# Bucketed attention and a feed-forward block on one core: an earlier row of maxima, a first operand loaded once, and conversions at other places

## The chip, the cores and the metric

The kernel runs on one core of a Trainium2 chip. Its engines work side by side and meet at semaphores: TensorE (PE, with its weight loads PEld), VectorE (DVE), ScalarE (ACT), GpSimd (POOL), and SyncE (SP), which here does nothing but issue DMAs. Each engine, and each DMA queue, takes its instructions in the order in which the program lists them. The metric is the device time of one execution in microseconds, lower is better.

## What is computed

Attention in which a query sees only the keys of its own hash bucket, and then a feed-forward block on its result:

```python
q, k, v: [4, 8, 768, 64] * 0.1;  proj: [64, 6];  w_in: [512, 2048];  w_out: [2048, 512]
bucket(x) = sum over n of 2**n * (x @ proj > 0)[n]
scores = where(bucket(q)[:, None] == bucket(k)[None], q @ k.T / 8, -1e9)
scores = scores - max(scores, -1);  attn = exp(scores)
attn = attn / (sum(attn) + 1e-9);   x = (attn @ v), as [4 * 768, 512]
h = x @ w_in
g = where(h >= 1, h, where(h <= -1, 0, (h + 1)**2 / 4))
out = g @ w_out
```

Everything is float32. Most products are made from two parts of the operands: a rounded high part and the low part that is left.

## The kernel before

**Two stages.** The first is attention over 32 heads (4 batches of 8), in 16 pairs that share tiles; the second is the feed-forward block (FFN).

**Units.** Each head has 12 units (`NU`): two halves of 384 queries by six blocks of 128 keys. The loop over `g` runs through 32 x 12 units. In unit `g` PE makes the scores of one block of keys (`s_unit`, lines 391 and 392: two matmuls, of which the second takes in the bucket bits and the row of maxima), ACT makes two exponentials of them (line 400 the rounded one `ph`, line 405 the exact one), DVE or POOL subtracts to get the low part `pl` (`lo_unit`, helper `sub` on line 39), and PE makes the products with V four units later (`LAG`, `pv_unit`, lines 424, 426 and 428). In between, PE makes the scores of a head two heads on for its maximum (`max_mm`, line 323; DVE reduces them in `max_red`, line 327).

**Three sets of tiles.** Pair `pr` uses `T1[pr % 3]` and `T2[pr % 3]`. What a pair needs is made in the even head two pairs ahead: `cast_h` and `low_h` (POOL) split the raw operand, `move` (four DMAs on SP, part 0 to 3) copies halves between partitions, `bits_mm` (PE, line 221) and `bits_cmp` (DVE) make the bucket bits, `bits_scale` (POOL) and `bits_put` (four DMAs) bring them to rows 0 to 6 of `T2`.

**The row of maxima.** Row 7 of `T2` holds each query's negated maximum, clamped. For head `hd + 2` it is made in head `hd + 1`: `max_clamp` (POOL, lines 357 and 359), `max_tr` (a PE transpose, line 368), `max_put` (an ACT copy to `te`, line 373, and two DMAs on SP, line 375 to `T2` and line 377 to `e_d` in DRAM). The first score unit of head `hd + 2` reads that row in its second matmul (line 392).

**Order.** Beside the units everything is put at a unit by hand: `at(g, fn, ...)` adds a task to unit `g`, tasks of one unit run in the order in which they were added, after the unit's own work. The weights' tasks are added first, then those of the first operand, then attention's. The loop over `hd` in `attention` adds the steps named above.

**Weights.** The weights come as 64-bit words and are turned into float32 by `word_steps` (a load; ACT's `rebias`; DVE's `tail`, `shifted` and `signed`). `conv` puts these at units. Those of `w_in` are turned into the blocks that the FFN needs during attention and stored in `wc`. Of the 16 blocks of `w_out` eleven are converted during attention too, stored in DRAM (`wd`, line 108) and fetched again (`get`, line 112), and five are converted in the FFN.

**The FFN** works in four blocks (batches) of 56 products (8 x 7, an algorithm with seven products in place of eight). Product `k` is six matmuls (line 960), then one step on DVE or ACT that sums it up, the activation (ACT lines 811, 812; DVE lines 817, 818, issued by `due(1, k)`), its high and low part (`g_hi`, `g_lo`), and matmuls with `w_out` from a queue (line 856). Tasks stand in `prep[k]` (ahead of the product's matmuls) and `post[k]` (behind them).

**The FFN's operand.** It is the attention's result, which goes to DRAM (`xd`) head by head, plus sum of V, normalized. For block 0 it is made during attention by three objects of class `FirstX`: `fx[0]` and `fx[1]` are the left and right half (192 columns each) of the even column blocks, `fx[2]` the odd ones at full width (384). Each has four pieces, each with these steps: `load` (a DMA of the raw piece, from `xd`), `rows` (two DMAs of the per-head rows, `er`), `fill` (one DVE instruction, line 743: row times `sv` plus raw), `norm` (POOL, line 748: times the second row), and then `sums`, `hi` and `lo`. For the later blocks `x_plan` places the same steps in the FFN.

## Time and profile before

| | before |
|---|---|
| time, median of 3 runs | 1008.0 us (1003.87 to 1008.73) |
| time of the profiled execution | 1006.24 us |
| its span, first to last instruction | 1004.4 us |
| mean granted clock of TensorE | 0.989 |
| busy: PE, PEld | 964.9 us (96%), 888.1 us (88%) |
| busy: DVE, ACT, POOL | 748.2 us (74%), 685.7 us (68%), 375.1 us (37%) |
| DMA | 174.37 MB in 85209 packets, 174 GB/s on average |

How to read the rows below: a row of a time line has the start and the duration in us, engine, source line, operation, and what is written from what (out<-in); SPq is the SP queue, whose rows are issues of DMAs, not their transfers; several alike in a row are merged (x3). In brackets stands how long the engine was idle before, and what ended that. A row of waits says who waited for whom: us in total, times, the longest. A row of windows has the window, its length, then the busy time of PE, PEld, DVE, ACT and POOL with their instruction counts, the granted clock, the busy share of the DMA engines and GB/s. Matmuls are pipelined: one is recorded about twice as long as the distance from one to the next. Attention lasts to about 490 us of the span; the FFN follows.

### The profile page before, as it was taken

What the parts mean: (1) busy time and instruction counts of PE and PEld (TensorE: products, weight loads), DVE (VectorE), ACT (ScalarE), POOL (GpSimd) and SP (SyncE); (2) the same over time, 40 slices, a digit from 0 to 9 for tenths busy, and PEclk for the clock granted to TensorE, in tenths of its full rate; (3) what the DMA queues carried; (4) which work ended last, traced back from release to release, by engine and by line L of the source; (5) the groups of instructions that cost most, each with busy time, mean ns of one, the idle gap of its engine ahead of it and who ended that gap; (6) DMA issues with size and microseconds to landing.
All of it is one profiled execution on the core that took longest, in us unless ns stands there. A gap on an engine that the chain in (4) does not pass through costs nothing.

```text
span 1004.4 us, 15651 instructions
## 1 busy us (share of the span) xinstructions
PE 964.9 (96%) x5002; PEld 888.1 (88%) x5002; DVE 748.2 (74%) x1311; ACT 685.7 (68%) x1510; POOL 375.1 (37%) x500
## 2 busy tenths in 40 slices
PE   8999999989999979989999999999999999999998
PEld 7899999988999979879888878888998889988896
DVE  8778888877888868878577898677766677755554
ACT  7889899978889968878655656545555454554444
POOL 8767778857779857876400000000000000000000
PEclk9999999989999989999999999999999999999999
DMA  6766766868776666664485764946448465454431
GB/s 165 188 170 169 207 182 174 250 179 248 199 202 166 184 212 175 186 205 136 144 228 167 217 218 126 260 134 195 118 134 245 133 179 148 134 168 116 116 105 63
DMA packets 85209, 174.37 MB, mean 174 GB/s; under 512 B 13524, under 2 KB 35656, under 8 KB 84104
## 3 DMA queue, kind: packets, MB, share of 16 engines
q1 hardware_dynamic: 84858, 173.34, 60.8%
q8 instruction: 40, 0.66, 0.3%
q14 instruction: 41, 0.34, 0.1%
q10 hardware_dynamic: 270, 0.04, 0.0%
HBM read 116.35 MB, written 30.46 MB: 146 GB/s over the span
## 4 chain that ended last, share of the span: by engine, by line
PE 68%; DVE 9%; ACT 9%; DMA 7%; issue 2%; POOL 1%; SPq 1%; ACTq 0%; DVEq 0%; POOLq 0%
PE y L856 23%; PE h L960 20%; DMA t<-te 5%; PE smax L323 5%; PE s L392 4%; PE o L424 4%; PE o L428 4%; PE o L426 4%; PE s L391 4%; ACT ph L400 2%; PE o L221 2%; DVE nm L327 2%; ACT pf L405 1%; ACT s L405 1%; DVE t L817 1%
## 5 line engine op out<-in xcount | busy, mean ns | idle before, releaser
L400 ACT ACTIVATE ph<-s 128x384 fp32r<-128x384 f32 x380 | 190.5, 501 | 52.0 <-PE s L392 45.3
L327 DVE TENSOR_REDUCE nm<-smax 128x1 f32<-128x768 f32 x189 | 180.2, 954 | 39.9 <-PE smax L323 38.8
L39 DVE TENSOR_TENSOR pl<-s,ph 128x384 fp32r<-128x384 f32 x256 | 138.8, 551 | 31.7 <-ACT s L405 27.5
L817 DVE SCALAR_TENSOR_TENSOR t<-t 128x384 f32<-128x384 f32 x128 | 71.4, 558 | 108.9 <-ACT z L812 108.8
L39 POOL TENSOR_TENSOR pl<-pf,ph 128x384 fp32r<-128x384 f32 x128 | 130.5, 1023 | 55.0 <-ACT pf L405 52.1
L392 PE MATMUL s<-t 128*128 128x384 f32 x384 | 132.3, 345 | 17.0 <-DMA t<-te 16.9
L424 PE MATMUL o<-ph,va 128*128 128x386 f32 x384 | 132.1, 344 | 5.1 <-DVE rw L83 4.9
L428 PE MATMUL o<-pl,va 128*128 128x386 f32 x384 | 131.7, 343 | 1.2 <-DVE pl L39 1.2
L391 PE MATMUL s<-t 128*128 128x384 f32 x384 | 132.0, 344 | 0.0
L426 PE MATMUL o<-ph,vb 128*128 128x386 f32 x384 | 131.6, 343 | 0.0
L405 ACT ACTIVATE s<-s 128x384 f32<-128x384 f32 x252 | 127.2, 505 | 0.0
L856 PE MATMUL y<-t,ghi 128*128 128x512 f32 x384 | 125.9, 395 | 0.0
L323 PE MATMUL smax<-t 128*128 128x384 f32 x378 | 101.5, 350 | 5.2 <-DVE nm L327 4.1
L822 ACT CAST ghi<-z 128x384 fp32r<-128x384 f32 x128 | 64.9, 507 | 39.9 <-DVE z L818 36.4
L392 PEld LDWEIGHTS s<-t 128*128 128x128 f32 x384 | 73.5, 192 | 21.0 <-DMA t<-te 20.8
L960 PE MATMUL h<-wbig,t 128*128 128x384 f32 x420 | 84.5, 337 | 0.8 <-DVE cu L979 0.8
L812 ACT ACTIVATE z<-t,m 128x384 f32<-128x384 f32 x128 | 79.0, 617 | 4.2
L960 PEld LDWEIGHTS h<-wbig,t 128*128 128x128 f32 x420 | 74.9, 188 | 7.3 <-DVE cu L979 1.9
L856 PEld LDWEIGHTS y<-t,ghi 128*128 128x128 f32 x384 | 71.5, 188 | 10.5 <-issue 0.2
L323 PEld LDWEIGHTS smax<-t 128*128 128x128 f32 x378 | 67.4, 192 | 14.6 <-DVE nm L327 12.4
L424 PEld LDWEIGHTS o<-ph,va 128*128 128x128 f32 x384 | 73.4, 191 | 6.7 <-issue 5.2
L856 PE MATMUL y<-woh,glo 128*128 128x512 f32 x192 | 76.0, 396 | 1.6 <-DVE glo L826 1.3
(180 smaller groups left out, 2044.1 us busy)
## 6 DMA issues: line engine op xcount, KB each, us to landing
t<-wc SPq DMA_DIRECT2D x140, 256.0 KB
t<-t SPq DMA_DIRECT2D x60, 384.0 KB
ring<-wc SPq DMA_DIRECT2D x84, 256.0 KB
raw<-in_qk_dram SPq DMA_DIRECT2D x14, 768.0 KB
wraw<-in_w_in_dram SPq DMA_DIRECT2D x16, 512.0 KB
wraw<-in_w_out_dram SPq DMA_DIRECT2D x16, 512.0 KB
wc<-wbig SPq DMA_DIRECT2D x8, 1024.0 KB
xd<-xs SPq DMA_DIRECT2D x32, 192.5 KB
```

The source lines that it names most:

```text
L39: eng.tensor_tensor(out=out, in0=a, in1=b, op=ALU.subtract)
L323: nc.tensor.matmul(out=smax[hd][:, hf, 0:HS], lhsT=t2[:, 0, h, i * P:(i + 1) * P], rhs=t2[:, 1, h, hf * HS:(hf + 1) * HS], start=True, sto ...
L327: nc.vector.tensor_reduce(out=nmp(hd)[:, i:i + 1], in_=smax[hd][:, :, 0:HS], axis=AX.XY, op=ALU.max, negate=True)
L391: nc.tensor.matmul(out=ps[:, 0:HS], lhsT=t1[:, 1, h, ks], rhs=t1[:, 0, h, sl], start=True, stop=False)
L392: nc.tensor.matmul(out=ps[:, 0:HS], lhsT=t2[:, 1, h, ks], rhs=t2[:, 0, h, sl], start=False, stop=True)
L400: nc.scalar.activation(out=ph[:, 0:HS], in_=ps[:, 0:HS], func=AF.Exp, scale=SCALE)
L405: nc.scalar.activation(out=pf, in_=ps[:, 0:HS], func=AF.Exp, scale=SCALE)
L424: nc.tensor.matmul(out=o, lhsT=wa, rhs=ph, start=(jj == 0), stop=False)
L426: nc.tensor.matmul(out=o, lhsT=wb, rhs=ph, start=False, stop=False)
L428: nc.tensor.matmul(out=o, lhsT=wa, rhs=pl, start=False, stop=(jj == NJ - 1))
L856: nc.tensor.matmul(out=ys[c][m], lhsT=g_[:, m * P:(m + 1) * P], rhs=w, start=(first and k == 0), stop=(last and k == 2))
L960: nc.tensor.matmul(out=ps, lhsT=w[:, cs], rhs=x, start=(n == 0 and s not in (2, 3, 6)), stop=(n == 5), skip_group_check=True)
```

## The change

In even heads (from head 4 on) the steps stand at other units: the transpose and the puts of the row of maxima one unit earlier (unit 6; in head 4 unit 5), the third and fourth cast one unit later, moves 0 and 1 at unit 6, behind the row's puts, move 2 at unit 8, the raw load at unit 9, the second bits product at unit 8, with what hangs on it one unit later. The bits' puts stay at unit 18.

`FirstX` is given tiles of its own for the raw pieces (`raw`: in `wbig` for `fx[0]` and `fx[1]`, in `T1` for `fx[2]`). `load` loads a raw piece in full width together with its rows; `fx[1]` loads nothing any more. `fill` is now an ACT instruction (row times `sv`), and `norm` has one more POOL instruction that adds the raw piece. The second and the fourth piece of `fx[0]` and `fx[1]` are filled two units later, and the four loads of `fx[2]` go from units 2 to 9 of head 28 to units 7, 9, 12 and 14 from its start, the fills to 12, 14, 17 and 19.

In `conv` the steps `tail` and `shifted` stand one unit later in odd heads above 3; the sums of a batch one unit later. In the FFN `due(1, k)` stands behind the product's own step for the first seven products, the conversions and fetches of `w_out` (blocks 2 to 15) stand at products given by a table, and four normalizations in blocks 1 and 3 one product later.

```diff
@@ -593,22 +593,23 @@
         pr, h = hd // 2, hd % 2
         g = hd * NU
         if 0 < hd < NH - 2:
-            gc, gt = ((30, 32), (41, 43))[hd - 1] if hd < 3 else (g + NU + SHIFT - 1, g + NU + SHIFT + 1 + 2 * h)
+            gc, gt = ((30, 32), (41, 43))[hd - 1] if hd < 3 else (g + NU + SHIFT - 1, g + NU + SHIFT + 1 + h * (hd > 3))
             at(gc, max_clamp, hd + 2, nc.gpsimd)
             at(gt, max_tr, hd + 2)
             at(gt, max_put, hd + 2)
         if h == 0 and pr + 2 < NPAIR:
             g0 = g + (13, 2)[pr] if pr < 2 else g
             for n in range(4):
-                gq = g0 + n + (pr == 1 and n == 3)
+                gq = g0 + n + (n == 3 if pr == 1 else n > 1 if pr > 1 else 0)
                 at(gq, cast_h, pr + 2, nc.gpsimd, n % 2, n // 2)
                 at(gq, low_h, pr + 2, nc.gpsimd, n % 2, n // 2)
+            gm = g0 + (3, 4, 6)[min(pr, 2)]
             for n in range(2):
-                at(g0 + 3 + (pr == 1), move, pr + 2, n)
-            at(g0 + 6, move, pr + 2, 2)
+                at(gm, move, pr + 2, n)
+            at(g0 + (8 if pr > 1 else 6), move, pr + 2, 2)
             if pr + 3 < NPAIR:
-                at(g0 + 7, load_raw, pr + 3)
-            bits_at = (((20, 1), (23, 0)), ((8, 1), (11, 0)))[pr] if pr < 2 else ((5, 1), (7, 1))
+                at(g0 + (9 if pr > 1 else 7), load_raw, pr + 3)
+            bits_at = (((20, 1), (23, 0)), ((8, 1), (11, 0)))[pr] if pr < 2 else ((5, 1), (8, 1))
             for hf, (n, bank) in enumerate(bits_at):
                 at(g + n, bits_mm, pr + 2, hf, bank)
                 at(g + n + 1, bits_cmp, pr + 2, hf)
@@ -727,24 +728,22 @@
     SUMS = {3: (3, 2, 3, ALU.add), 5: (2, 0, 2, ALU.subtract), 4: (0, 3, 0, ALU.subtract), 6: (1, 1, 0, ALU.subtract)}
     HOME = (0, 1, 3, 3, 0, 2, 1)
 
-    def __init__(self, nc, xm, cc, sl, pc, er, home, sv):
-        self.nc, self.xm, self.cc, self.sl, self.pc, self.er, self.home, self.sv = nc, xm, cc, sl, pc, er, home, sv
+    def __init__(self, nc, xm, cc, sl, pc, raw, er, home, sv):
+        self.nc, self.xm, self.cc, self.sl, self.pc, self.raw = nc, xm, cc, sl, pc, raw
+        self.er, self.home, self.sv = er, home, sv
 
     def load(self, k):
-        a = k // 2 * CH
-        self.nc.sync.dma_start(out=self.pc(k), in_=self.xm.x_d[0][:, 2 * (k % 2) + self.cc,
-                                                                 a + self.sl.start:a + self.sl.stop])
-
-    def rows(self, k):
-        self.xm.load_rows(0, 2 * (k % 2) + self.cc, k // 2, self.er[k])
+        ct, a = 2 * (k % 2) + self.cc, k // 2 * CH
+        self.nc.sync.dma_start(out=self.raw[k], in_=self.xm.x_d[0][:, ct, a:a + CH])
+        self.xm.load_rows(0, ct, k // 2, self.er[k])
 
     def fill(self, k):
-        r, er, ct = self.pc(k), self.er[k][:, 0, self.sl], 2 * (k % 2) + self.cc
-        self.nc.vector.scalar_tensor_tensor(out=r, in0=er, scalar=self.sv()[:, ct, 0:1], in1=r, op0=ALU.mult,
-                                            op1=ALU.add)
+        self.nc.scalar.activation(out=self.pc(k), in_=self.er[k][:, 0, self.sl], func=AF.Copy,
+                                  scale=self.sv()[:, 2 * (k % 2) + self.cc, 0:1])
 
     def norm(self, k):
         r = self.pc(k)
+        self.nc.gpsimd.tensor_tensor(out=r, in0=r, in1=self.raw[k][:, self.sl], op=ALU.add)
         self.nc.gpsimd.tensor_tensor(out=r, in0=r, in1=self.er[k][:, 1, self.sl], op=ALU.mult)
 
     def sums(self, o, eng):
@@ -919,7 +918,7 @@
             x_plan(b, 1, n + 34, range(n + 26, n + 34, 2), [n + m for m in (37, 39, 43, 44)],
                    [n + m for m in (46, 47, 48, 50, 51, 53, 54)])
         else:
-            x_plan(b, 0, n + 9, range(n + 9, n + 21, 3), [n + m for m in (15, 18, 22, 25)],
+            x_plan(b, 0, n + 9, range(n + 9, n + 21, 3), [n + m for m in (16, 19, 23, 26)],
                    [n + m for m in (28, 30, 31, 32, 34, 35, 37)])
             x_plan(b, 1, n + 39, range(n + 30, n + 38, 2), [n + m for m in (43, 44, 46, 48)],
                    range(n + 49, n + 56))
@@ -945,7 +944,7 @@
         b, i, s = k // 56, k % 56 // NBLK, k % NBLK
         blk, o, bank = PRODUCTS[s]
         ps = hb[(bank + i) % 2][:, 0:CH]
-        for n in (3, 2, 1):
+        for n in (3, 2, 1) if k > 6 else (3, 2):
             due(n, k)
         if k > 0:
             w_load(k - 1 + NRING)
@@ -989,6 +988,7 @@
                 queue_out(*u)
                 if last and b < B - 1:
                     queue_out(*held)
+        due(1, k)
         for fn, a in post.pop(k, ()):
             fn(*a)
         issue(0 if k < 6 else 6 if s == 6 else 5)
@@ -1041,8 +1041,8 @@
         tasks[g].append((fn, a))
 
     def conv(g, steps, offs):
-        for fn, n in zip(steps, offs):
-            at(g + n, fn)
+        for i, (fn, n) in enumerate(zip(steps, offs)):
+            at(g + n + (i in (2, 3) and n > 7 and g // NU % 2 == 1 and g // NU > 3), fn)
 
     attn = {}
 
@@ -1127,23 +1127,27 @@
     for b in range(B - 1):
         g = (b + 1) * H * NU + LAG + 4
         at(g, lambda b=b: xm.sums_load(*(attn["small"].tile([P, NF], F32, name=n, bufs=1) for n in ("sm", "em")), b))
-        at(g + 29, xm.sums_add)
-        at(g + 29, xm.sums_inv, b)
+        at(g + 30, xm.sums_add)
+        at(g + 30, xm.sums_inv, b)
 
     def rows(t):
         return [t[:, 2 * k * CH:(2 * k + 2) * CH].bitcast(F32).rearrange("p (t n) -> p t n", t=2) for k in range(4)]
 
-    raw = []
-
-    def piece_raw(k):
-        if not raw:
-            raw.append(attn["work"].tile([P, 2, S], F32, name="raw", bufs=1).rearrange("p a (b n) -> p (a b) n", n=CH))
-        return raw[0][:, k]
-
-    fx = [FirstX(nc, xm, cc, sl, pc, er, lambda o, t, cc=cc: cut(wbig, 2 * NBLK * cc + 2 * o + t), lambda: attn["sv"])
-          for cc, sl, pc, er in ((0, slice(0, CH // 2), lambda k: xq[:, k], rows(wbig)),
-                                 (0, slice(CH // 2, CH), lambda k: xq[:, k], rows(wbig)),
-                                 (1, slice(0, CH), piece_raw, rows(flat(T2[i0]))))]
+    def four(t, n):
+        return [cut(t, n + k).bitcast(F32) for k in range(4)]
+
+    wide = []
+
+    def piece_wide(k):
+        if not wide:
+            wide.append(attn["work"].tile([P, 2, S], F32, name="raw", bufs=1).rearrange("p a (b n) -> p (a b) n", n=CH))
+        return wide[0][:, k]
+
+    fx = [FirstX(nc, xm, cc, sl, pc, raw, er, lambda o, t, cc=cc: cut(wbig, 2 * NBLK * cc + 2 * o + t),
+                 lambda: attn["sv"])
+          for cc, sl, pc, raw, er in ((0, slice(0, CH // 2), lambda k: xq[:, k], four(wbig, 8), rows(wbig)),
+                                      (0, slice(CH // 2, CH), lambda k: xq[:, k], four(wbig, 8), rows(wbig)),
+                                      (1, slice(0, CH), piece_wide, four(flat(T1[i0]), 0), rows(flat(T2[i0]))))]
 
     def load_sv():
         attn["sv"] = attn["small"].tile([P, NCT, 2], F32, name="xsv0", bufs=1)
@@ -1161,10 +1165,8 @@
     at(unit(10, 8), load_sv)
     for k, (h, n) in enumerate(((11, 6), (11, 9), (13, 6), (13, 9))):
         at(unit(h, n), fx[0].load, k)
-        at(unit(h, n), fx[0].rows, k)
-        at(unit(22, 9), fx[1].load, k)
-    for n, gs in enumerate((((13, 1, 5), (13, 1, 7), (15, 1, 5), (15, 1, 10)),
-                            ((23, 1, 5), (23, 1, 7), (25, 1, 4), (25, 1, 5)))):
+    for n, gs in enumerate((((13, 1, 5), (13, 3, 7), (15, 1, 5), (15, 3, 10)),
+                            ((23, 1, 5), (23, 3, 7), (25, 1, 4), (25, 3, 5)))):
         for k, (h, a, m) in enumerate(gs):
             at(unit(h, a), fx[n].fill, k)
             at(unit(h, m), fx[n].norm, k)
@@ -1172,11 +1174,10 @@
                               ((2, 25, 6), (0, 25, 8), (1, 25, 10), (3, 27, 9), (5, 28, 0), (4, 28, 3), (6, 28, 7)))):
         for o, h, m in plan:
             piece(fx[n], o, unit(h, m), nc.scalar, nc.gpsimd)
-    for k, n in enumerate((12, 13, 17, 20)):
-        at(g0 + 2 + 2 * k, fx[2].load, k)
-        at(g0 + 3 + 2 * k, fx[2].rows, k)
-        at(g0 + n - (k != 1), fx[2].fill, k)
-        at(g0 + n, fx[2].norm, k)
+    for k, (n, a, m) in enumerate(((7, 12, 13), (9, 14, 15), (12, 17, 18), (14, 19, 20))):
+        at(g0 + n, fx[2].load, k)
+        at(g0 + a, fx[2].fill, k)
+        at(g0 + m, fx[2].norm, k)
     for o, n in ((0, 23), (2, 24), (1, 26), (3, 28), (5, 31), (4, 34), (6, 37)):
         if o in FirstX.SUMS:
             at(g0 + n, fx[2].sums, o, nc.vector)
@@ -1191,18 +1192,21 @@
     for i in range(len(wo), NFT):
         woh.append(wp2.tile([P, DM], F32R, name=f"woh{i}"))
         wol.append(wp2.tile([P, DM], F32R, name=f"wol{i}"))
-    for f in range(2, NFT):
-        need = NBLK * (f // 2) + (4 if f % 2 == 0 else 6)
+    starts = dict(zip(range(2, NFT), (1, 2, 6, 7, 11, 12, 17, 22, 27, 16, 23, 30, 32, 37)))
+    for f, n in sorted(starts.items(), key=lambda x: x[1]):
         if f in late:
             get, back = late[f]
-            prep[need - 8].append((get, ()))
+            prep[n].append((get, ()))
+            n_cast, n_low = n + 3, n + 4
         else:
-            back, steps = ws.word_steps(wout_v[f], (P, DM, 2), ws.square)
-            for fn, m in zip(steps, (12, 7, 7, 6, 5)):
-                (prep if m == 12 else post)[need - m].append((fn, ()))
+            back, (s0, *steps) = ws.word_steps(wout_v[f], (P, DM, 2), ws.square)
+            prep[n - 5].append((s0, ()))
+            for fn, m in zip(steps, (0, 0, 1, 3)):
+                post[n + m].append((fn, ()))
+            n_cast, n_low = n + 4, n + 6
         cast, low = ws.split(back, woh[f], wol[f], nc.scalar, nc.vector)
-        post[need - 4].append((cast, ()))
-        post[need - 3].append((low, ()))
+        post[n_cast].append((cast, ()))
+        post[n_low].append((low, ()))
     areas = [flat(t) for t in (T2[i0], T2[i1], T1[i0])], wbig
     ffn(ctx, tc, woh, wol, xm, areas, ring, wst, wc, out, prep, post)
 
```

## The prediction

> **What bounds the kernel now.** I read the page, the waits of TensorE (PE) in the attention stage, the time lines of PE and of the SP queue round one long wait, the clock by windows, and ACT's share in the last heads.
>
> ```profile
> PE 964.9 (96%) x5002; PEld 888.1 (88%) x5002; DVE 748.2 (74%) x1311; ACT 685.7 (68%) x1510; POOL 375.1 (37%) x500
> ...
> PE s L392 <- DMA t<-te: 16.9, 10, 3.9
> PE o L424 <- DVE rw L83: 4.9, 1, 4.9
> ...
> 132.00:159.10 27.10, 27.10 (x156) 26.59 (x156) 22.78 (x36) 24.76 (x61) 21.28 (x28) 1.00 0.79 220
> 187.80:220.90 33.10, 29.69 (x155) 29.12 (x154) 24.54 (x39) 25.85 (x63) 22.56 (x29) 0.90 0.71 203
> ```
>
> PE is the bound: the pair of heads 8 and 9 (132.0 to 159.1 us) has 156 matmuls in 27.10 us with no idle, 0.174 us each. The pair 12 and 13 needs 33.10 us for 155. What differs is ten waits for the row of maxima (t<-te), one wait behind DVE, and the clock. A matmul is recorded 0.34 us long but starts every 0.174 us, so each listed wait hides another 0.17 us: the ten are worth 16.9 + 1.7 = 18.6 us, the one 5.1 us.
>
> ```profile
> 318.20 2.43 SPq L174 DMA_DIRECT2D t<-t  x3
> 320.73 1.53 SPq L375 DMA_DIRECT2D t<-te  x1
> ...
> 319.50 0.22 PE L368 MATMUL s<-ident_r,nmr 128*12 128x128 f32 x1
> 319.56 0.91 PE L221 MATMUL o<-t,pw 128*128 128x384 f32 x4
> ...
> 324.53 0.34 PE L391 MATMUL s<-t 128*128 128x384 f32 x1
> 325.53 0.44 PE L392 MATMUL s<-t 128*128 128x384 f32 x1 [0.67 <-DMA t<-te]
> ...
> 201.58 0.79 SPq L375 DMA_DIRECT2D t<-te  x1
> ...
> 205.71 0.69 PE L392 MATMUL s<-t 128*128 128x384 f32 x1 [3.41 <-DMA t<-te]
> ```
>
> Head 20 shows the pattern. The transpose L368 runs at 319.50, the row's put goes out at 320.73, behind three moves of the pair, and head 21's second score matmul starts at 325.53, 4.8 us after the put. In head 12 the put went out at 201.58, when head 13's score was already due, and landed 4.1 us later. The wait follows the put's time.
>
> ```profile
> 204.59:211.41 6.82, 5.70 (x18) 5.71 (x19) 2.82 (x5) 2.88 (x7) 1.00 (x1) 0.50 0.92 261
> 296.75:300.16 3.41, 3.41 (x12) 3.41 (x11) 2.84 (x6) 1.87 (x5) 1.62 (x2) 0.50 1.01 299
> 361.60:368.43 6.83, 4.06 (x13) 3.90 (x14) 5.16 (x9) 1.34 (x4) 3.25 (x6) 0.50 0.60 198
> 450.35:453.76 3.41, 3.41 (x11) 3.41 (x12) 1.17 (x2) 1.40 (x4) 1.00 (x1) 0.50 1.02 311
> ```
>
> After the four longest waits the granted clock was 0.50 (last three columns: clock, DMA share, GB/s). What PE lost there while it worked is its busy time less count x 0.174: 5.70 - 3.13, 3.41 - 2.09, 4.06 - 2.26, 3.41 - 1.91, together 7.2 us.
>
> **The change part by part.**
>
> *Row of maxima.* In even heads from 4 on the transpose, ACT copy and two puts (row and e_d) go from unit 7 to 6 (head 4: to 5), the pair's moves 0 and 1 from unit 3 to 6 behind them, move 2 from 6 to 8, the raw load from 7 to 9, move 3 from 8 to 9. No instruction is added. A unit is about 1.1 us, so head 20's put goes out at 319.50 - 1.1 + 1.2 = 319.6, and its row is due at 324.70. That leaves 5.1 us.
>
> ```profile
> 142.34 0.78 SPq L375 DMA_DIRECT2D t<-te  x1
> ...
> 146.41 0.34 PE L392 MATMUL s<-t 128*128 128x384 f32 x1
> ```
>
> A put behind the moves landed within 4.1 us here (head 9 did not wait), 4.8 us in head 20, so 5.1 us is enough even there; ahead of the moves it can only be shorter. In head 12 a weight put (wd) still stands ahead of the row, and I leave 0.3 us of wait. Behind the put on SP now stand the moves, about 1.3 us later; the next reader, the pair's bits, is next. Move 3, the raw load (next read 15 units on) and the bits' put (still at unit 18) have units to spare: nothing.
>
> *Casts, clamp, bits.* The third and fourth casts go a unit later on POOL, the clamp now stands ahead of the third, and the second bits product goes from unit 7 to 8.
>
> ```profile
> 317.28 0.23 POOL L357 TENSOR_SCALAR nmr<-nm 128x6 fp32r<-128x6 f32 x1
> ...
> 318.26 1.02 POOL L39 TENSOR_TENSOR t<-raw,t 128x384 fp32r<-128x384 f32 x1
> 319.23 1.99 POOL L39 TENSOR_TENSOR pl<-pf,ph 128x384 fp32r<-128x384 f32 x2
> ```
>
> The clamp comes up to 1.5 us earlier, so the earlier transpose does not wait. One low part pl (1.0 us) now stands ahead of the fourth cast: its low part ends at 319.28 + 1.0 = 320.3, and the bits product, 319.56 before, comes at about 320.7. Margin 0.4 us; I leave 0.3 us in all.
>
> *First operand.* Loaded once at full width, so the four loads in head 22 and 23 go; scaling goes from DVE to ACT, adding the raw piece to POOL.
>
> ```profile
> 356.89 4.48 SPq L735 DMA_DIRECT2D xq<-xd  x4
> ...
> 356.89 5.44 DMA xq<-xd
> ...
> 363.57 0.67 DVE rw L83
> ...
> L743 DVE SCALAR_TENSOR_TENSOR xq<-wbig,xsv,xq 128x192 f32<-128x192 f32 x8 | 3.0, 414 | 5.2 <-DMA xq<-xd 5.2
> L743 DVE SCALAR_TENSOR_TENSOR raw<-t,xsv,raw 128x384 f32<-128x384 f32 x4 | 2.5, 617 | 0.0
> L755 ACT CAST wbig<-xq 128x192 fp32r<-128x192 f32 x14 | 5.1, 363 | 0.3 <-POOL xq L748 0.3
> L755 ACT CAST wbig<-raw 128x384 fp32r<-128x384 f32 x7 | 3.7, 533 | 1.8 <-DVE raw L752 1.8
> L748 POOL TENSOR_TENSOR xq<-xq,wbig 128x192 f32<-128x192 f32 x8 | 4.8, 600 | 0.0
> L748 POOL TENSOR_TENSOR raw<-raw,t 128x384 f32<-128x384 f32 x4 | 4.0, 1007 | 3.5 <-DVE raw L743 3.0 <-PE o L426 0.5
> ```
>
> The 5.1 us wait is this: the second loads went out at 356.89, landed 5.44 us later, DVE stood at the first fill, and PE waited for a DVE operation queued behind it. Without the load there is no such wait: -5.1 us. DVE loses 8 x 0.414 + 4 x 0.617 = 5.8 us, POOL gains 8 x 0.600 + 4 x 1.007 = 8.8 us of its idle time, ACT gains 8 x 0.363 + 4 x 0.533 = 5.0 us: bounds for ACT are nothing and these casts, which have the same shapes.
>
> The Trainium skill ("ScalarE: Activation LUTs", Rules for kernel authors) speaks against this: multiplications belong on VectorE, and an ACTIVATE takes about 0.3 us plus 0.83 ns per element. By that estimate the fills would take 8 x 0.46 + 4 x 0.62 = 6.2 us, and the sum would come out 0.4 us worse by the four in head 29. The cast rows above are lower, and I go by them.
>
> Where ACT has no room is the tail, heads 28 to 31:
>
> ```profile
> 432.30:446.10 13.80, 13.31 (x75) 12.55 (x74) 12.41 (x19) 13.60 (x36) 12.16 (x18) 1.00 0.66 192
> 446.10:464.50 18.40, 14.52 (x75) 14.13 (x74) 13.50 (x22) 11.59 (x29) 9.11 (x11) 0.91 0.81 232
> 464.50:477.10 12.60, 11.85 (x67) 11.17 (x67) 10.38 (x16) 11.44 (x31) 9.28 (x11) 1.00 0.29 83
> 477.10:489.00 11.90, 11.43 (x63) 10.64 (x62) 7.78 (x13) 11.17 (x29) 9.16 (x10) 1.00 0.15 41
> ```
>
> Head 29 without its wait (4.1) and half clock (1.5) is 12.8 us; ACT there would be busy 11.59 + 4 x 0.533 = 13.7 us. So 0.9 us comes back. The third operand's loads also move from units 2 to 9 of head 28 to units 7 to 14, and their fills now stand in ACT's queue ahead of the next exponentials. If one waits for its rows, exp waits, then the scores. The bounds are 0 and the 5.4 us that the late load above took; DVE took these fills without a wait for data, and each has five units, so I take 0.6 us. Tail: +1.5 us.
>
> *Clock.* All four intervals follow waits that go: -7.2 us. The Trainium skill ("TensorE: Matmul & The Clock Gate", Part 1 and HAM oscillation) has the clock drop only after idle gaps over about 3.4 us, in a free-running window of that length. The trace agrees on the length (3.41 and 6.83 us), but the interval at 296.75 follows a wait of only 2.1 us:
>
> ```profile
> 293.50 0.34 PE L391 MATMUL s<-t 128*128 128x384 f32 x1
> 295.74 0.44 PE L392 MATMUL s<-t 128*128 128x384 f32 x1 [1.90 <-DMA t<-te]
> ```
>
> By the rule that interval would not be the wait's, and 1.3 us of the 7.2 would stay. I go by the row.
>
> *FFN.* For the first seven products the activation's two DVE steps go behind the product's own DVE step; the second weight's conversions are done earlier, all five full ones by product 43; four normalizations of blocks 1 and 3 go one product later.
>
> ```profile
> 520.00:551.40 31.40, 31.40 (x157) 28.14 (x156) 24.05 (x46) 15.95 (x30) 0.00 (x0) 1.00 0.63 179
> 578.30:609.70 31.40, 29.56 (x143) 25.22 (x142) 29.64 (x57) 18.84 (x36) 0.00 (x0) 1.00 0.58 191
> ...
> PE h L960 <- DVE cv L971: 0.9, 1, 0.9
> ```
>
> From 578.3 to 609.7 PE made 143 matmuls where a steady stretch makes 157: 14 x 0.2 = 2.8 us, with DVE busy 29.64 of 31.40. Conversions moved ahead go into a stretch where DVE is busy 24.05 of 31.40; three of them at some 2.6 us (estimate from L83's 0.67 us, four operations) fit, but tightly, so I count 2.0 of the 2.8. The reordered start takes away L971's wait, 0.9 + 0.17 = 1.0 us, unless the earlier reads of the converted weights hold ACT (0 to 1.5 us). FFN: -3.0, bounds +1 and -4.
>
> Conversion steps and sums moved by one unit: same counts, read two or more units later: nothing.
>
> **Sum.** -18.6 - 5.1 - 7.2 - 3.0 + 1.5 + 0.3 + 0.3 = -31.8 us. The profiled execution took 1006.24 us (its span 1004.4); the median of three runs is 1008.0 (1003.87 to 1008.73). 1006.2 - 31.8 gives 974.4; I say 974.5.
>
> **Rivals.**
> 1. *ACT takes over the tail* (0.10). A fill waits for its rows the full 5.4 us instead of 0.6, and a half-clock interval of 1.5 us follows. For: DMA runs at 232 GB/s in head 29, and all four loads now lie later. Against: the old loads had the row's put queued among them. 974.5 + 6.3 = 981.
> 2. *The row is still late in the backlogged heads* (0.10). Half of the waits stay (9.3), with half clock at 204, 296 and 450 (2.6 + 1.3 + 1.5). For: 204.59's window moves 261 GB/s. Against: the put is earlier there too. 989.
> 3. *The wait is not the row's* (0.05). L392 reads the whole tile, which moves and bits also write; if one of those ended the waits, only 5.1 + 1.8 + 3.0 - 1.5 = 8.4 us come: 998. Against: the wait followed the put by 4.1 and 4.8 us.
> 4. *Slower* (0.03). The fourth cast stands behind pl, which waits for ACT's exp. If its low part is late, PE waits at the second bits product in each of the twelve even heads 4 to 26. The margin is 0.4 us; 31.8 / 12 = 2.65 us beyond it, 3.1 us in each head, eats the whole gain, 3.5 us in each makes 1011 or more. Against: POOL ran on without a gap there, and its work is the same.
> 0.02 remain for no change.
>
> **Numbers.** My forecast has 0.70, with 968 to 979. With the first two rivals the range is 967 to 990, which covers FFN's bounds and the tail's. A measurement of this kernel tells about 0.5% (5 us) from no change: faster 0.95, same 0.02, slower 0.03.
>
> **What would show it.** Right: no wait of L392 for t<-te above a few tenths; t<-te issued ahead of t<-t in even heads; clock 1.00 from 60 to 480 us; the attention stage some 29 us shorter; no xq<-xd after head 13; 157 matmuls in the FFN stretch after product 40. Wrong: PE idle before L221 for POOL, before L391 or L424 for ACT in heads 28 to 31, or the clock at 0.50 again.

## The result and the profile after

The changed kernel takes 994.2 us (median of 4 runs, 993.24 to 998.12) against 1006.37 us (4 runs, 1003.87 to 1008.73) for the kernel before in the same comparison: ratio 0.9887, 95% interval 0.9847 to 0.9926. It is faster, clear of the noise, by 12 us where 32 were forecast, and outside the range. The profiled execution took 994.74 us, its span 993.0 us, 11.4 us less than the span before. One run of the last experiment below took 2398.71 us where its nine others took 1002.89 to 1006.83 us, and is left out of the numbers there.

Where these 11.4 us lie can be read from the starts of each head's first score matmul (L391) on PE's time line; a head's length is the distance to the next head's start. The sums are over the heads named, and the forecast column sorts the prediction's terms into the same rows.

| | before | after | measured | forecast |
|---|---|---|---|---|
| start to head 0 | 12.2 | 12.0 | -0.2 | 0 |
| heads 0 to 3 | 63.7 | 63.5 | -0.2 | 0 |
| even heads 4 to 26 | 175.2 | 191.3 | +16.1 | +0.3 |
| odd heads 5 to 27 | 181.2 | 157.2 | -24.0 | -25.1 |
| heads 28 to 31 | 58.7 | 59.0 | +0.3 | -4.0 |
| FFN | 513.5 | 510.0 | -3.5 | -3.0 |

The odd heads and the FFN did what was forecast. Nearly the whole miss is in the even heads, for which almost nothing was forecast, and in the last four heads. The waits of PE from head 4 to head 27 show it, first of the kernel before, then of the changed one (who waited for whom, us in total, times, longest):

```profile
PE s L392 <- DMA t<-te: 13.1, 9, 3.4
PE o L424 <- DVE rw L83: 4.9, 1, 4.9
PE smax L323 <- DVE nm L327: 2.0, 4, 0.8
```

```profile
PE smax L323 <- DVE nm L327: 8.9, 14, 1.1
PE s L392 <- DMA t<-te: 4.1, 3, 2.1
PE o L424 <- DVE neg L232: 2.3, 12, 0.2
PE o L428 <- DVE pl L39: 0.7, 3, 0.3
```

Nine waits for the row became three, and not the same ones: those before stood in odd heads, these stand in heads 12, 18 and 24. The wait for L83 is gone. New are ten waits for the reduction of the maxima and one in each even head for `neg`, the comparison that makes the bucket bits.

**Unit 2 of the even heads.** DVE's time line in head 20, first before, then after (start, duration):

```profile
309.18 0.69 DVE L76 TENSOR_SCALAR o<-wraw 128x512 int32<-128x512 int32 x1 [0.31 <-ACT xs L434]
309.79 0.95 DVE L327 TENSOR_REDUCE nm<-smax 128x1 f32<-128x768 f32 x1
```

```profile
308.03 0.69 DVE L76 TENSOR_SCALAR o<-wraw 128x512 int32<-128x512 int32 x1
308.62 0.55 DVE L39 TENSOR_TENSOR pl<-s,ph 128x384 fp32r<-128x384 f32 x1
309.09 0.75 DVE L79 SCALAR_TENSOR_TENSOR o<-rw,wsc,o 128x512 int32<-128x512 int32 x1
309.75 0.95 DVE L327 TENSOR_REDUCE nm<-smax 128x1 f32<-128x768 f32 x1
...
310.75 0.62 PE L323 MATMUL smax<-t 128*128 128x384 f32 x2 [1.08 <-DVE nm L327]
```

Before, `tail` (L76) stood in DVE's idle time at the end of head 19, and `shifted` (L79) behind the next reduction. After, both run in the first units of head 20, ahead of the reduction whose `smax` buffer PE's next maximum needs: PE stands for 1.08 us.

**Unit 10.** Later in head 20 PE stands again (DVE's time line, then PE's):

```profile
318.68 0.95 DVE L327 TENSOR_REDUCE nm<-smax 128x1 f32<-128x768 f32 x1
319.54 0.55 DVE L39 TENSOR_TENSOR pl<-s,ph 128x384 fp32r<-128x384 f32 x1
320.01 0.54 DVE L232 TENSOR_TENSOR neg<-o,neg 32x384 f32<-32x384 f32 x1
```

```profile
320.05 0.33 PE L392 MATMUL s<-t 128*128 128x384 f32 x1
320.60 0.45 PE L424 MATMUL o<-ph,va 128*128 128x386 f32 x1 [0.21 <-DVE neg L232]
```

The second bits product now goes at unit 8, so its comparison (L232) runs at 320.01 to 320.55. It reads the PSUM bank `o` in which the second half's products with V begin, and these wait for it.

**The rows of heads 12, 18 and 24.** SP's queue, ACT's copy of the row and PE round head 18:

```profile
260.21 1.22 SPq L1079 DMA_DIRECT2D wc<-wbig  x1
...
264.99 0.95 SPq L174 DMA_DIRECT2D t<-t  x1
265.98 0.58 SPq L158 DMA_DIRECT2D raw<-in_qk_dram  x1
...
269.56 0.47 SPq L174 DMA_DIRECT2D t<-t  x1
270.08 0.58 SPq L66 DMA_DIRECT2D wraw<-in_w_out_dram  x1
...
273.23 0.78 SPq L375 DMA_DIRECT2D t<-te  x1
```

```profile
270.81 0.25 ACT L373 CAST te<-s 12x128 fp32r<-12x128 f32 x1
```

```profile
278.56 0.44 PE L392 MATMUL s<-t 128*128 128x384 f32 x1 [2.07 <-DMA t<-te]
```

The row left at 273.23, though ACT's copy of it was done at 271.06, and PE read it 5.3 us later. Those 5.3 us are not the lateness: the rows of heads 13 and 21 in the kernel before took 4.1 and 4.8 us. What is late is the issue. Move 2 now goes out (264.99) behind a put of 1 MB (L1079). Move 3 overwrites what move 2 reads, so SP stands at it until move 2 has landed, issues it at 269.56, and comes to the row last. The rows of heads 12 and 24 left 3.2 and 2.7 us after their copies. What SP waited for in the whole run, first before, then after:

```profile
SPq L174 <- DMA t<-t: 17.4, 11, 2.6
```

```profile
SPq L174 <- DMA t<-t: 47.0, 15, 5.3
```

**Head 29.** ACT, POOL and PE:

```profile
444.93 0.61 ACT L741 ACTIVATE raw<-t,xsv 128x384 f32<-128x384 f32 x1 [2.75 <-DMA t<-ed]
```

```profile
445.62 0.99 POOL L746 TENSOR_TENSOR raw<-raw,t 128x384 f32<-128x384 f32 x1 [2.31 <-DMA wraw<-in_w_out_dram]
446.70 0.99 POOL L747 TENSOR_TENSOR raw<-raw,t 128x384 f32<-128x384 f32 x1
447.66 0.23 POOL L357 TENSOR_SCALAR nmr<-nm 128x6 fp32r<-128x6 f32 x1
```

```profile
448.13 0.23 PE L368 MATMUL s<-ident_r,nmr 128*12 128x128 f32 x1 [3.00 <-POOL nmr L359]
```

The first operand's fill (L741) waits for its rows, POOL's add (L746) for the fill, which ended at 445.54 (the row names a transfer that ended about then), the clamp (L357, L359) stands behind POOL's two instructions, and PE's transpose waits for the clamp. Then the clock falls, the only time between 60 us and the FFN (last three columns: clock, DMA share, GB/s):

```profile
448.40:451.80 3.40, 3.40 (x12) 3.40 (x12) 1.39 (x2) 2.04 (x6) 3.03 (x4) 0.50 0.82 228
60.00:448.00 388.00, 367.99 (x2046) 352.60 (x2044) 318.00 (x487) 343.51 (x842) 308.93 (x396) 1.00 0.71 200
```

### The profile page after: what moved, and what is told of

Same layout as the page of the kernel before. It is cut to its first block, busy times and chain, and to the rows that moved or that the text cites. A ratio compares the mean times of both kernels' runs of the same rounds, so it can differ in the third digit from the quotient of the medians.

```text
span 993.0 us, 15666 instructions
## 1 busy us (share of the span) xinstructions
PE 960.1 (97%) x5002; PEld 881.9 (89%) x5002; DVE 743.0 (75%) x1299; ACT 687.2 (69%) x1522; POOL 383.8 (39%) x512
## 4 chain that ended last, share of the span: by engine, by line
PE 67%; DVE 10%; ACT 9%; POOL 4%; issue 4%; DMA 3%; SPq 0%; ACTq 0%; DVEq 0%; POOLq 0%
PE y L855 24%; PE h L959 21%; PE smax L323 4%; PE o L424 3%; PE o L428 3%; PE o L426 3%; PE s L391 3%; PE s L392 3%; DVE nm L327 3%; ACT ph L400 3%; DVE pl L39 2%; ACT s L405 1%; PE o L221 1%; POOL pl L39 1%; DMA wraw<-in_w_out_dram 1%
## 5 line engine op out<-in xcount | busy, mean ns | idle before, releaser
L327 DVE TENSOR_REDUCE nm<-smax 128x1 f32<-128x768 f32 x189 | 180.1, 953 | 29.8 <-PE smax L323 28.1
L391 PE MATMUL s<-t 128*128 128x384 f32 x384 | 131.8, 343 | 1.2 <-DVE pl L39 1.2
L392 PEld LDWEIGHTS s<-t 128*128 128x128 f32 x384 | 72.6, 189 | 5.4 <-DMA t<-te 5.3
L391 PEld LDWEIGHTS s<-t 128*128 128x128 f32 x384 | 72.5, 189 | 4.3 <-DVE pl L39 2.0
```

Of the source, the lines that this page charges most:

```text
L327: nc.vector.tensor_reduce(out=nmp(hd)[:, i:i + 1], in_=smax[hd][:, :, 0:HS], axis=AX.XY, op=ALU.max, negate=True)
L391: nc.tensor.matmul(out=ps[:, 0:HS], lhsT=t1[:, 1, h, ks], rhs=t1[:, 0, h, sl], start=True, stop=False)
L392: nc.tensor.matmul(out=ps[:, 0:HS], lhsT=t2[:, 1, h, ks], rhs=t2[:, 0, h, sl], start=False, stop=True)
```

## The experiments

Theory A: each new wait belongs to one moved step and has its own price, so prices add. Theory B: DVE, POOL or the DMA engines are used up, and a wait taken away here comes back elsewhere. Kernels below differ from the changed kernel unless the text says from the one before. "us" are medians, with the ratio to the kernel before on the same chip. The kernel before took 1004.58 to 1006.37 us in the different comparisons, so a difference of 2 us between two experiments says little by itself.

**Conversion steps back** (`tail`, `shifted` at the units of before).

```diff
-            at(g + n + (i in (2, 3) and n > 7 and g // NU % 2 == 1 and g // NU > 3), fn)
+            at(g + n, fn)
```

> The changed kernel, with the two conversion steps tail and shifted back at their old units in odd heads. Theory A (each new wait has a place of its own): the wait of the maxima's scores for DVE's reduction at unit 2 of the even heads, 10.1 us over heads 4 to 27 in the changed kernel and 2.5 before, falls to 2 to 4 us, the even heads get some 0.5 us shorter each, and the time falls by 6 to 8 us, to 987. Theory B (DVE and POOL are used up once PE no longer stalls, so a wait taken away returns elsewhere): time within 2 us of the changed kernel's 994, with the wait at another unit.

988.82 us, ratio 0.9847 [0.9817, 0.9877]. Head 8 goes from 15.24 to 14.70 us, head 20 from 15.94 to 15.38, head 22 from 16.14 to 15.57: 0.55 us a head. PE's waits for L327 fall to 3.8 us (2.0 in the kernel before). It is not the same in every even head: 4, 14, 18 and 24 gain 0.2 us or nothing, and the twelve are 4.7 us shorter together. Head 29 goes the other way, from 17.82 to 19.16 us, with the clock at half for 6.8 us. Theory A for the most part.

**Casts and second bits product back** (move 3 stays).

```diff
-                gq = g0 + n + (n == 3 if pr == 1 else n > 1 if pr > 1 else 0)
+                gq = g0 + n + (pr == 1 and n == 3)
-            bits_at = ... else ((5, 1), (8, 1))
+            bits_at = ... else ((5, 1), (7, 1))
```

> The changed kernel, with the third and fourth cast and the second bits product (and its comparison) of the even heads back at their old units, and move 3 left where the change put it. Theory A: the wait of L424 for DVE's comparison at unit 10 of the even heads (5.5 us over heads 4 to 27 with what follows it) goes, the time falls by 4 to 6 us, to 989; the wait at unit 2 stays. If the casts mattered for the transposes, L368 now waits for POOL's clamp at unit 6. Theory B: within 2 us of 994.

994.51 us, ratio 0.9905 [0.9869, 0.9941]: no gain, a miss. Yet the waits at unit 10 are gone and head 8 is 0.53 us shorter, head 22 0.43. The rows took it back: the waits for t<-te rose from 4.1 to 7.1 us, with an interval at half clock behind one of them (profile of this kernel):

```profile
PE s L392 <- DMA t<-te: 7.1, 4, 2.6
...
278.50:281.90 3.40, 3.40 (x13) 3.40 (x12) 2.44 (x5) 1.76 (x5) 3.24 (x5) 0.50 0.94 311
```

**Move 2 at unit 7**, one step ahead on SP's queue, as a first guess at why these rows are late; and then **move 2 and the raw load at unit 7**.

```diff
-            at(g0 + (8 if pr > 1 else 6), move, pr + 2, 2)
+            at(g0 + (7 if pr > 1 else 6), move, pr + 2, 2)
```

> The changed kernel, with move 2 one unit earlier in even heads (unit 7 in place of 8), so that it stands ahead of what SP takes at unit 8 (the batch sums' loads, the load of sv, weights' puts). Theory A: the late rows of heads 12, 18 and 24 (waits of 1.4, 2.2 and 1.0 us at their first score) come from SP standing in the odd head before at move 3, which waits for move 2 to land; they go, the time falls by 3 to 5 us, to 990. Theory B: the three waits stay, or DVE's wait at unit 2 of the same heads takes their place (none stands there in heads 12 and 18 now): 993 to 995.

```diff
-                at(g0 + (9 if pr > 1 else 7), load_raw, pr + 3)
+                at(g0 + 7, load_raw, pr + 3)
```

> The changed kernel with move 2 and also the raw load at unit 7 of the even heads, so that the raw operand (768 KB) goes out ahead of the loads that wait at unit 8 and not in the odd head ahead of the next row. In the run with move 2 alone at unit 7 head 12's row was put earlier (185.0 us) and landed later, behind the raw load that had been issued at 178.2. Theory A2 (the raw load's place is what makes the rows of heads 12, 18 and 24 late): the three waits go, 4 to 5 us less than the changed kernel, 989 to 990. Theory A1 (it is SP's standing at move 3): as with move 2 alone, no gain, 994 or above.

1000.98 us (0.9956 [0.9931, 0.9982]) and 996.38 us (0.9913 [0.9888, 0.9937]). The first is slower than the changed kernel, the second no better; the rows' waits were 6.3 and 5.6 us where the changed kernel has 4.1. Both guesses fell, but not because SP's standing was misread. With move 2 alone at unit 7 the rows of heads 12, 18 and 24 left within 0.9 us of their copies, and then took 7.9, 6.2 and 6.9 us to their readers, with the put and the raw load issued ahead of them. The lateness moved from the issue to the transfer, so the order of these transfers among themselves is not the remedy.

**The tail's loads earlier**, all four at unit 7 of head 28.

```diff
-    for k, (n, a, m) in enumerate(((7, 12, 13), (9, 14, 15), (12, 17, 18), (14, 19, 20))):
+    for k, (n, a, m) in enumerate(((7, 12, 13), (7, 14, 15), (7, 17, 18), (7, 19, 20))):
```

> The changed kernel, with all four loads of the third operand at unit 7 of head 28, still behind the row, ahead of the weight put and the weight load that now stand between them. Theory A: head 29's long wait (3.2 us at L368 for POOL's clamp, behind a POOL addition that waits for its data) is the loads' lateness; it goes, ACT's 3.2 us of waiting for the rows too, head 29 is 14 to 15 us in place of 17.8, and the time falls by 3 to 4 us, to 990.5. Theory B: ACT and POOL are full in heads 28 to 31, their sum stays at 59 us: 993 to 995.

991.61 us, ratio 0.9871 [0.9841, 0.99]. Head 29 falls from 17.82 to 13.95 us, head 30 rises from 13.33 to 14.13, heads 28 to 31 are 3.1 us shorter together; the clock does not fall. The wait of head 29 is now

```profile
PE s L368 <- POOL nmr L359: 0.5, 1, 0.5
```

So the data of the fill was late, not ACT or POOL too slow.

**All four together** (conversions, casts and bits, move 2 and raw load, tail's loads):

> The changed kernel with four places put right together: conversion steps back, third and fourth cast and second bits product back, move 2 and the raw load at unit 7 of the even heads, the third operand's loads all at unit 7 of head 28. Theory A (the gain was lost at separate places): the parts add, 5 for the conversions, 5 for the bits, 4 for the rows and 3 for the tail: 976 to 978, with no wait of L392 for the row over 1 us, and the even heads within 0.4 us of their length before. Theory B (DVE's queue is the next bound once PE runs on): the waits for DVE gather at units 0 and 2 of the even heads instead, and the time stays at 984 or above.

984.44 us, ratio 0.9793 [0.9769, 0.9818]. The time is theory B's, the mechanism is not: the waits for L327 from 100 to 490 us fell from 9.9 to 4.7 us. The even heads without a late row are mostly as before (head 8 14.16, head 22 15.21; head 14 is not, 15.85 against 14.22, with a wait for L327 of 1.07), but PE still waits for the rows of heads 12, 18 and 24. Head 18 in this kernel: SP, what SP waited for at the row, PE, and windows from the put to the row.

```profile
260.61 1.57 SPq L1079 DMA_DIRECT2D wc<-wbig  x1
...
270.28 0.77 SPq L375 DMA_DIRECT2D t<-te  x1
...
SPq L375 <- DMA wc<-wbig: 1.5, 1, 1.5
...
275.29 0.44 PE L392 MATMUL s<-t 128*128 128x384 f32 x1 [1.85 <-DMA t<-te]
...
260.30:268.00 7.70, 7.70 (x45) 7.49 (x45) 7.22 (x12) 7.55 (x21) 4.95 (x8) 1.00 0.95 277
...
276.30:279.70 3.40, 3.40 (x12) 3.40 (x11) 2.63 (x5) 2.08 (x6) 3.24 (x5) 0.51 0.94 316
```

The DMA engines are busy 0.95 of the time at 277 GB/s ahead of the row, and SP does not stand at move 3 here, but at the row itself, by the profile until the put has landed. Heads 12, 18 and 24 follow those in which the weights put 1 MB of `w_in`'s blocks into `wc` (heads 10, 16, 22). That gave theory D: the backlog makes the row late, and this put, which nothing reads before the end of attention, is what can leave it.

**The put 12 units later**, first with the four repairs, then alone.

```diff
-            puts, shis, slos = (44, 56), (42, 43), (44, 46)
+            puts, shis, slos = (44, 68 if p < 7 else 56), (42, 43), (44, 46)
```

> The four-part kernel (conversion steps, casts and bits product, move 2 and raw load, the tail's loads at other units), and besides the second put of w_in's blocks into wc, 1 MB, in heads 10, 16 and 22 taken 12 units later, behind the row of maxima instead of ahead of it (head 28 stays). Theory D (the rows of heads 12, 18 and 24 are late because the DMA engines work off a backlog in which this put stands, at 277 GB/s and 0.95 share): the three waits of 1.47, 2.01 and 0.82 us go and with them the half clock at 276.3, so heads 12, 14, 18 and 24 come back to about 14.3 to 15.2 us; 979 to 981 us against 984.4. Theory E (the row is late through what its own queue or ACT does, the put is not in its way): the waits stay, 983.5 to 985.5 us.

> The changed kernel with the same put 12 units later and nothing else. Theory D: the waits at heads 12, 18 and 24 (1.40, 2.23, 1.00 us) go, the waits for VectorE at units 2 and 10 stay: 989 to 990.5 us against 994.2. Theory E: 993.5 to 995 us.

978.86 us (0.9744 [0.971, 0.9777]) with the repairs, 990.4 us (0.9857 [0.9826, 0.9888]) alone: theory D both times, in that the put is what makes the rows late. Alone, heads 12, 18 and 24 go from 49.98 to 45.53 us together; move 2 goes out 1.8 to 2.0 us earlier ahead of each of these heads, their rows leave within 0.1 us of their copies and take no more than 5.5 us. Head 29 gains 1.8, mostly because the clock does not fall behind its wait. In the first the row of head 18 leaves SP at 265.25 with the put behind it, PE's waits from head 4 to 27 and the clock over the whole stage are

```profile
265.25 0.78 SPq L375 DMA_DIRECT2D t<-te  x1
...
270.15 0.82 SPq L1079 DMA_DIRECT2D wc<-wbig  x2
...
PE smax L323 <- DVE nm L327: 3.9, 9, 0.8
...
PE s L392 <- DMA t<-te: 0.6, 1, 0.6
...
60.00:480.00 420.00, 409.72 (x2285) 393.36 (x2285) 348.51 (x541) 381.14 (x930) 334.08 (x422) 1.00 0.71 201
```

and head 18 takes 14.18 us. This version beats both kernels.

**Put later, casts and bits product back**, to see whether the second experiment's gain had been eaten by the rows.

> The changed kernel with the second bits product, its comparison and the third and fourth casts back at their old units, and with the put of w_in's blocks 12 units later. Theory A (the waits at unit 10, 5.5 us, were worth their time all along; alone their removal gained nothing because the rows of heads 12, 18 and 24, behind the put, were then late by as much more): with the put out of the way the even heads are 0.45 us shorter each and no row is late, 985 to 986 us against 990.4 with the put alone. Theory B (the stall at unit 10 covers something else, which comes late in its turn): 989 to 991 us.

988.61 us, ratio 0.9835 [0.9816, 0.9853]. No row is late by more than 0.3 us, and heads 4 to 27 together are 4.4 us shorter than with the put alone (even heads -5.4, odd heads +1.0): A, as far as these heads go. The total misses A's 985 to 986 and is not clear of the noise against the put alone, because head 29, untouched here, takes 18.23 instead of 16.03 us: its wait for the clamp is 3.5 us instead of 2.7, and the clock falls behind it. Why that wait grew was not tried.

**From the kernel before: only the row and moves 0 and 1.**

```diff
-... else (g + NU + SHIFT - 1, g + NU + SHIFT + 1 + 2 * h)
+... else (g + NU + SHIFT - 1, g + NU + SHIFT + 1 + h * (hd > 3))
-                at(g0 + 3 + (pr == 1), move, pr + 2, n)
+                at(g0 + (3, 4, 6)[min(pr, 2)], move, pr + 2, n)
```

> The kernel before with one thing alone: the row of maxima at its new unit, and moves 0 and 1 behind it at unit 6 (casts, bits, conversions, first operand and FFN as before). Theory A: the row's waits before the odd heads (18.6 us with the hidden part) and three of the four half-clock intervals (5.4) go, nothing comes in their place in the even heads: some 983 to 986. The wait for the first operand in head 23 stays. Theory B: the even heads get longer here too, by about 1 us each, and the time is 993 or above.

998.16 us, ratio 0.9927 [0.9905, 0.9949], a miss. The even heads 4 to 26 grew by 6.8 us, nearly all of it in heads 8, 12 and 18, which waited for their rows: theory B for these. So the new places of the row and of moves 0 and 1 are enough to make rows of even heads late. The odd heads' rows up to head 27 came in time, but head 23 went from 21.16 to 24.94 us: the wait for the first operand grew as the row's went, and half clock with it. The wait for the rows from head 4 to 27, PE in head 23, and the window there:

```profile
PE s L392 <- DMA t<-te: 4.7, 4, 2.0
...
360.38 0.66 PE L424 MATMUL o<-ph,va 128*128 128x386 f32 x1 [9.08 <-DVE rw L83]
...
356.20:366.40 10.20, 6.02 (x19) 5.87 (x20) 5.18 (x9) 2.21 (x6) 4.51 (x7) 0.50 0.47 147
```

The row's gain in head 23 needs the first operand's load gone as well.

**The reverse: the changed first operand and FFN without the attention steps.**

```diff
-... SHIFT + 1 + h * (hd > 3))
+... SHIFT + 1 + 2 * h)
-            gm = g0 + (3, 4, 6)[min(pr, 2)]
+            gm = g0 + 3 + (pr == 1)
...
```

> The changed kernel without its attention steps: row of maxima, moves, casts, bits product and conversion steps at the units of the kernel before; the first operand (with its tail) and the FFN as changed. The odd heads' waits for the row (16.9 us) come back except where a stall covers them. Theory A (each part has its own price): head 23 without the load's wait and the half clock behind it is 6 to 7 us shorter, the FFN 3.3, the tail 4 to 6 us longer: 1000 to 1002 us against 1005.8. Theory B (the freed time falls to the next wait): head 23 then waits for its row instead and gives back 3 us or more: 1004 to 1006 us.

1000.57 us, ratio 0.9952 [0.993, 0.9974]. Head 23 takes 14.10 us, 7.1 less than before, though PE waits 1.09 us for its row again, and no even head waits for its row. Theory A.

**From the kernel before: only the conversion steps' shift**, the first experiment's edit the other way round.

```diff
-            at(g + n, fn)
+            at(g + n + (i in (2, 3) and n > 7 and g // NU % 2 == 1 and g // NU > 3), fn)
```

> The kernel before with the conversion steps' shift alone. Theory A: tail and shifted now run at the start of the even heads, and the even heads' wait at unit 2 for DVE grows by 0.5 us or more each; as the even heads have no other wait, the time grows by 4 to 7 us over the kernel before. Theory B (the shift costs only where PE no longer stalls): even heads as before within 0.2 us each, time within 2 us of before.

1004.28 us (median of nine), ratio 0.9999 [0.9983, 1.0016]. The waits of PE from head 4 to 27 in this kernel:

```profile
PE smax L323 <- DVE nm L327: 7.5, 11, 1.1
PE o L424 <- DVE rw L83: 6.2, 1, 6.2
PE s L392 <- DMA t<-te: 6.1, 9, 1.6
```

Against the kernel before, L327 costs 5.5 us more and the row 7.0 us less. The shift stalls PE as it does in the changed kernel; here the stall comes ahead of a row that is late anyway and gives it the time to land: the even heads are 6.7 us longer, the odd ones 8.5 us shorter. So in the kernel before the shift is free, and with an early row it has a price.

## Why the prediction was half right

*Row of maxima, -18.6.* Right for the rows that it looked at: no odd head waits for t<-te, and these heads gained 24.0 us where the row, the load and the clock came to 25.1. What failed is the sentence that what stands behind the row has "units to spare: nothing". It priced move 3 and the raw load by their own readers, and left out that SP takes its issues in order. Move 2 now goes out behind the put, SP stands at move 3 until it has landed (47.0 us in the run where it was 17.4), and the next row, that of the even head, leaves 2.2 to 3.2 us late in three heads. Cost: three waits, 4.1 us listed, 4.6 with 0.17 each. Moving one put by 12 units removes them. Rival 2 named this kind of lateness but in the odd heads.

*Conversion steps: "nothing".* This step failed: it compared the moved steps with their own readers. The price is at another instruction: the reduction that stands behind it on DVE, about 0.55 us in most even heads by the first experiment, 4.7 us in the twelve.

*Casts, clamp, bits: 0.3.* The margin was worked out for the product L221, and that does not wait. What was not followed is the bank that the product writes: it is free only when the comparison L232 is done, and the products with V begin in it at unit 10. Some 0.45 to 0.53 us a head by the second experiment, 5.4 us in the twelve once no row is late. Taken away one after the other, the put (191.3 to 187.1 us for the even heads), the casts and bits product (to 181.7), and then the conversion steps, with move 2, the raw load and the tail's loads (to 176.6), leave 1.4 of the even heads' 16.1 us. The odd heads become 1.9 us longer on this way, 157.2 to 159.1.

*First operand, -5.1, and clock, -7.2.* Right: head 23 fell by 7.1 us with the load alone, which is 5.1 and the 1.8 of its interval, and all four intervals are gone. The one new interval follows the new wait of head 29. By the rule of the Trainium skill ("TensorE: Matmul & The Clock Gate", HAM oscillation), that only idle gaps over about 3.4 us cost the clock, the interval at 296.75 would have stayed. It went with its wait, and with all four repairs one came behind a wait of 1.85 us. The changed kernel's own wait of 2.07 us had none behind it, nor had one of 3.05 us with move 2 alone at unit 7; the runs do not show what decides.

*Tail, +1.5.* It came to +5.8: 0.3 in the table, where -4.0 holds this 1.5 already. The late loads are 3.1 of it, by the experiment that issues them earlier. About 0.9 is the conversion steps' price in heads 28 and 30, which fell by 0.56 and 0.29 in the first experiment. The rest, 1.8, is near the 1.5 that was forecast; what it consists of was not tried. The wait for the rows was 3.2 us in all, inside the bounds of 0 to 5.4 and far from the 0.6 taken, and it was followed to ACT's exponentials alone. The longer way is the one that set the time: fill, POOL's two instructions, clamp, transpose, then half clock. That is near rival 1's size (6.3), and begins with its late rows, but the way to PE is by POOL. The fills themselves took longer than the casts I priced them by:

```profile
L741 ACT ACTIVATE xq<-wbig,xsv x8: 440/460/496, 207.8 to 386.6; 128x192 f32<-128x192 f32 x8
L741 ACT ACTIVATE raw<-t,xsv x4: 600/608/615, 440.1 to 452.1; 128x384 f32<-128x384 f32 x4
```

The median is 0.460 and 0.608 us (middle figures, ns), not 0.363 and 0.533. The Trainium skill ("ScalarE: Activation LUTs", Rules for kernel authors) gives 0.46 and 0.62 by the estimate quoted in the prediction; here the page was nearer than my rows of another operation.

*FFN, -3.0.* Right, -3.5. The stretch after product 40 has 154 matmuls in 31.40 us where it had 143 and 157 were named as the sign, and DVE has room in it:

```profile
568.40:599.80 31.40, 31.07 (x154) 27.29 (x153) 25.59 (x51) 16.53 (x32) 0.00 (x0) 1.00 0.55 163
```

With the four repairs and the put later, 978.86 us was reached, 4.4 above the forecast and 25.7 below the kernel before of that comparison, where 31.8 were forecast. So most of the gain that was counted could be had; the change gave nearly two thirds of it back in places that were set to nothing or to little.

## What to carry to other kernels

A long wait is time that every other queue uses: before it is counted as gain, look for what is late next, on the same and on each other engine, in the queue that issues the DMAs, and in the DMA engines' backlog. A step moved by one unit is priced at the instruction that stands behind it on its in-order engine and at the buffer that it holds, not by the slack of its own reader. And a small transfer with a due time should not queue behind a large one without: moving three puts of 1 MB that nothing reads for long took 3.8 us off the changed kernel and 5.6 off its repaired form.

## What was not expected of the hardware

A put of 1 MB that nothing reads for long made a transfer of 3 KB late in two ways. In the changed kernel it delayed an earlier move, and with it SP, which issued the row 2.2 to 3.2 us after its data was ready. With move 2 issued earlier the row left in time and took 6.2 to 7.9 us from issue to its reader's start, in place of at most 5.5 us where the put was moved behind it. The Trainium skill ("DMA: Bandwidth & Descriptors", Queues, rings and completion order) says that on each DMA engine the descriptors of one ring are consumed in ring order; these longer transfers agree with that. Adding a stall to PE can be free: 5.5 us of new waits for DVE left the time at ratio 0.9999.
